# Gate and up of a SwiGLU MLP in seven block products in place of eight, with the output product as a phase of its own

## The chip, the cores and the metric

The kernel runs on one core of one Trainium2 chip. The metric is device time in microseconds (us), as the median of several executions. Beside it stands one profiled execution, from which all durations of single instructions come. Engines are named as in the profile: PE is TensorE (matmuls), PEld its weight load, DVE VectorE, ACT ScalarE, POOL GpSimd and SP SyncE, which here issues DMAs. Each engine takes its instructions in a fixed order; an instruction that waits holds up all behind it on the same engine. Code is written for a scheduler that keeps the order of the program on each engine and moves an instruction only past others that aren't ready.

## The reference, cut to what matters

The input u has L = 2048 tokens of D = 640. Of its two blocks, the first (layer norm, modulation, an S4 convolution by FFT, residual) is not touched by the change. The second is layer norm, modulation and an MLP with F = 1728:

```python
mod = (_silu(c) @ w_mod).reshape(c.shape[0], 6, 1, -1)
sa, ca, ga, sb, cb, gb = ...
x = x + ga * _A_ref(h, ...)                      # the convolution block
h = _layernorm(x, axis=-1) * (1 + cb) + sb
gate = jnp.einsum("bsd,df->bsf", h, w1)          # 640 -> 1728
up = jnp.einsum("bsd,df->bsf", h, w3)
out = jnp.einsum("bsf,fd->bsd", _silu(gate) * up, w2)
x = x + gb * out
```

## The kernel before

**Stages.** The first block takes the start of the execution; at its end the convolution's result lies in DRAM as `zs`. Then comes the MLP, in four quarters q of 512 tokens, each four tiles `xm` of 128 tokens x 640.

**Precision.** Every product of the MLP is three fp32r products: an operand is split into a high part (a cast on ACT) and a low part (operand less high part, on DVE), and hi·hi, hi·lo and lo·hi are added in PSUM (`prod3`, L964 to L969). `split` (L946 to L954) does it for weights and h: ACT's cast is L952, DVE's subtraction L953.

**One f-tile of a quarter** (`mlp`, L986). F is cut in 14 f-tiles: 13 of 128 columns, and f = 13, which holds the last 64 columns of w1 and of w3 side by side. For each, wg, wu and w2 (320 KB each) are loaded by SP (`weight`, L956; `w_get`, L651 and L653), again in each quarter; wg and wu are split (tiles gh, gl, uh, ul); w2 is multiplied with the modulation vector `gbr` on POOL (L1000) and split (wh, wl). Gate `pg` and up `pu` are 15 matmuls each of 128x512 (five blocks of 128 along D, three products each; only `pg` for f = 13), in PSUM pool `psG` of three banks. Then ACT takes silu (L1024), DVE multiplies (`hf`, L1025), and h is split (`hh`, `hl`). `outstep` (L971) multiplies h with w2: 15 matmuls at L981 (10 for f = 13, whose two halves lie on separate partitions), added up over all f in five banks `acc` of pool `psA`. The outstep of f-tile f-1 stands behind gate and up of f-tile f, so its inputs have the time of gate and up to be made. First of all f-tile 0 of quarter 0 orders its products by x's high and low parts (L1009).

**Preparation of the next quarter.** `prep` is a generator; `mlp` takes one step of it per f-tile. Steps are, per tile, `x_mid` (L902): z and x loaded by SP (five z issues, L638, one x issue), eight small matmuls (L914), two additions from PSUM on DVE (L917), the norm's statistics on DVE (L126, L127, L129) and square root on POOL (L131, L132), normalising on DVE (`xn`, L920). Then per 128-block of D, `x_t` (L927): four transposes (L931), ACT's modulation (`xf`, L938) and cast (`xh`, L939), DVE's low part (`xl`, L941). Quarter 0 is prepared by `x_first` (L874), ahead of which TensorE does some matmuls on zeros (`keep_warm`, L868).

**End of a quarter.** `finish` (L1037) runs inside the last outstep: ACT scales acc[4] (`o`, L1040), DVE adds the accumulators to xm (L1043), four transposes (L1047) and four small additions (L1050), and SP stores the tiles (`x_out`).

**What sets the order.** Each engine's queue follows the program, with the scheduler's moves; `issue_after` adds a dependence by hand, `ends` and `last_sum` among them. The room for tiles comes from pools with a fixed number of buffers: two of every weight tile and of every part.

Of the kernel before, what the change touches and what calls it, by code (L numbers as in the profile page):

```python
# [92 lines left out]
def tile_kernel(ctx: ExitStack, tc: tile.TileContext, a):  # L93
# [5 lines left out]
    zs = dram.tile([NDC, NB, 2, NA, DC], F32, name="zs")  # L99

# [539 lines left out]
    def x_tiles(j):  # L640
        return xp.tile([P, D], F32, name=f"xm{j % 4}"), z_tile()
# [7 lines left out]
    def w_get(w, f, name):  # L649
        if name != "w2":  # L650
            nc.sync.dma_start(w, a[name][f])  # L651
        elif f < NFT - 1:
            nc.sync.dma_start(w, a["w2"][f * P:f * P + P, :])  # L653
# [99 lines left out]
    first_w = dict.fromkeys(("wg", "wu", "w2"))  # L753
# [73 lines left out]
    for tk in range(NS + 1, LAG + 8 * NDC + 2):  # L827
# [6 lines left out]
        if tk == NS + 1:  # L834
            tabs.close()
            xp = ctx.enter_context(tc.tile_pool(name="xp", bufs=2))

            xp.tile([P, 8], F32, name="shift_by", bufs=1)
            idle = xp.tile([P, 512], F32R, name="idle", bufs=1)
            G.memset(idle.bitcast(F32), 0.0)  # L840
            for j in range(4):
                early[j] = (xp.tile([P, D], F32, name=f"xm{j}"), early[j][1],
                            xp.tile([P, KD, 6], F32, name="st5", bufs=4))
# [6 lines left out]
    for name in first_w:  # L850
        first_w[name] = xp.tile([P, D] if name == "w2" else [P, KD, P], F32, name="e" + name, bufs=1)
        with tc.issue_after(i1_last[0].ins):
            w_get(first_w[name], 0, name)
# [3 lines left out]
    wq = ctx.enter_context(tc.tile_pool(name="wq", bufs=2, side="right"))  # L857
    mp = ctx.enter_context(tc.tile_pool(name="mp", bufs=2, side="right"))
# [4 lines left out]
    def side_bank(q):  # L863
        return (psG if q else psA).tile([P, 512], F32, name="ps", tag="g" if q else "acc")
# [3 lines left out]
    def keep_warm(n):  # L868

        ps = psA.tile([P, 512], F32, name="ps", tag="acc")  # L870
        for _ in range(n):
            tc.keep_in_program_order(PE.matmul(ps, idle[:, :P], idle, start=True, stop=True))

    def x_first(tiles):  # L874

        keep_warm(IDLE[0])
        pl = psA.tile([P, 4, P], F32, name="pl", tag="acc")
# [15 lines left out]
        V.scalar_tensor_tensor(rs[:, 2, :], mv[:, :, 0], -1.0, rs[:, 1, :], op0=OP.mult, op1=OP.mult)  # L893
        for j, (x, z, st) in enumerate(early):
            xn = xp.tile([P, D], F32, name=f"xn{j}", bufs=1)
# [4 lines left out]
            tiles.append((x, xn))  # L900

    def x_mid(q, tiles):  # L902

        for i in range(4):
            x, z = x_tiles(4 * q + i)
            with tc.issue_after(zlast[0].ins):
                z_load(z, 4 * q + i, range(NDC))
                nc.sync.dma_start(x, a["x"][(4 * q + i) * P:(4 * q + i + 1) * P, :])
            py = [side_bank(q) for _ in range(2)]
            for b in range(4):  # L910
                for hh in range(2):
                    r, c = slice(hh * 64, hh * 64 + 64), slice(b * NA, b * NA + NA)
                    n = ZW[hh]
                    PE.matmul(py[hh][c, :n], i2[r], z[r, b, :n], start=True, stop=True, tile_position=(r.start, c.start))  # L914
            for hh in range(2):
                h = slice(hh * 256, hh * 256 + ZW[hh])
                V.tensor_tensor(x[:, h], py[hh][:, :ZW[hh]], x[:, h], op=OP.add)  # L917
            mean, rstd = ln_stats(xp, x)
            xn = xp.tile([P, D], F32, name=f"xn{i}", bufs=1)
            V.tensor_scalar(xn, x, mean, rstd, op0=OP.subtract, op1=OP.mult)  # L920
            tiles.append((x, xn))
            yield
            yield
# [3 lines left out]
    def x_t(q, tiles, outs):  # L927
        for k in range(KD):
            px = side_bank(q)
            for i in range(4):  # L930
                PE.transpose(px[:, i * P:(i + 1) * P], tiles[i][1][:, k * P:(k + 1) * P], ident)  # L931
            xf = xp.tile([P, 512], F32, name="xf")
            xh = xp.tile([P, 512], F32R, name=f"xh{k}")
            if q == 0 and k % 2 == 0:
                ends[0] = S.activation(xh, px, AF.Identity, scale=modT[:, 1, k:k + 1], bias=modT[:, 0, k:k + 1])
                V.tensor_scalar(xf, px, modT[:, 1, k:k + 1], modT[:, 0, k:k + 1], op0=OP.mult, op1=OP.add)
            else:
                S.activation(xf, px, AF.Identity, scale=modT[:, 1, k:k + 1], bias=modT[:, 0, k:k + 1])  # L938
                ends[0] = S.copy(xh, xf)  # L939
            xl = xp.tile([P, 512], F32R, name=f"xl{k}")  # L940
            ins = V.tensor_tensor(xl, xf, xh.bitcast(F32), op=OP.subtract)  # L941
            ends[1] = ins
            outs.append((xh, xl))
            yield

    def split(pool, src, shape, name, after=None):  # L946
        hi = pool.tile(shape, F32R, name=name + "h")
        lo = pool.tile(shape, F32R, name=name + "l")
        with ExitStack() as order:
            for ins in after or ():  # L950
                order.enter_context(tc.issue_after(ins.ins))
            S.copy(hi, src)  # L952
            V.tensor_tensor(lo, src, hi.bitcast(F32), op=OP.subtract)  # L953
        return hi, lo  # L954

    def weight(q, f, name):  # L956
        if (q, f) == (0, 0):
            return first_w[name]
        w = wq.tile([P, D] if name == "w2" else [P, KD, P], F32, name=name)
# [4 lines left out]
    def prod3(ps, pairs):  # L964
        n = len(pairs)
        for i, ((wh, wl), (xh, xl)) in enumerate(pairs):
            PE.matmul(ps, wh, xh, start=(i == 0), stop=False)  # L967
            PE.matmul(ps, wh, xl, start=False, stop=False)  # L968
            PE.matmul(ps, wl, xh, start=False, stop=(i == n - 1))  # L969

    def outstep(acc, h, w2, f, done=None):  # L971

        if f < NFT - 1:
            terms = [(h[1], w2[0]), (h[0], w2[0]), (h[0], w2[1])]
        else:

            terms = [(h, w2[0]), (h, w2[1])]
        for k in (4, 0, 1, 2, 3):
            for i, (hh, w) in enumerate(terms):
                lhs, rhs = (hh[:, k * P:(k + 1) * P], w[:, :512]) if k < 4 else (w[:, 512:], hh)  # L980
                PE.matmul(acc[k], lhs, rhs, start=(f == 0 and i == 0),  # L981
                          stop=(f == NFT - 1 and i == len(terms) - 1))
# [3 lines left out]
    def mlp(q, tiles, xt, side):  # L986
        acc = None
        prev = None
        for f in range(NFT):
            last = f == NFT - 1  # L990

            after = ends if (q, f) == (0, 1) else last_sum if (q, f) == (0, 0) else None
            wr = weight(q, f, "wg")
            wgs = split(wq, wr, [P, KD, P], "g", after)
            if not last:
                wr = weight(q, f, "wu")
                wus = split(wq, wr, [P, KD, P], "u", after)
            w2r = weight(q, f, "w2")
            with tc.issue_after(zlast[1].ins):
                G.tensor_tensor(w2r[:, :512], w2r[:, :512], gbr, op=OP.mult)  # L1000
            w2s = split(wq, w2r, [P, D], "w", after)
            pg = psG.tile([P, 512], F32, name="pg", tag="g")
            if (q, f) == (0, 0):
                pu = psG.tile([P, 512], F32, name="pu", tag="g")
                for lo in range(2):
                    for k in range(KD):
                        for ps, ws in ((pg, wgs), (pu, wus)):
                            for i in range(1 if lo else 2):
                                PE.matmul(ps, ws[i][:, k, :], xt[k][lo], start=(k + i + lo == 0),  # L1009
                                          stop=(lo == 1 and k == KD - 1))  # L1010
            else:
                prod3(pg, [((wgs[0][:, k, :], wgs[1][:, k, :]), xt[k]) for k in range(KD)])
            if not last and (q, f) != (0, 0):
                pu = psG.tile([P, 512], F32, name="pu", tag="g")
                prod3(pu, [((wus[0][:, k, :], wus[1][:, k, :]), xt[k]) for k in range(KD)])
            if prev is not None:
                if acc is None:
                    acc = [psA.tile([P, 512], F32, name=f"acc{k}", tag="acc") for k in range(KD)]
                outstep(acc, *prev)
            next(side, None)  # L1020
            sg = mp.tile([P, 512], F32, name="sg")
            hf = mp.tile([P, 512], F32, name="hf")
            if not last:
                S.activation(sg, pg, AF.Silu)  # L1024
                V.tensor_tensor(hf, pu, sg, op=OP.mult)  # L1025
                hs = split(mp, hf, [P, 512], "h")
            else:
# [101 lines left out]
```

## Time and profile before

| what | value |
|---|---|
| device time, median of 3 | 1024.65 us |
| lowest and highest of them | 1022.72 and 1025.35 us |
| the profiled execution's own time | 1019.66 us |
| span of that execution in the profile | 1017.5 us |
| mean granted TensorE clock | 0.959 |
| first outstep of the MLP starts | 447.22 us into the span |
| last outstep of the MLP starts | 1005.62 us into the span |

The profile's page has the busy time of each engine first, then the chain of work that ended last, followed back from the last instruction. A view by windows gives, for each stretch of time, the busy time and the number of instructions of each engine, the granted clock, the share of time in which the DMA engines were busy and what they moved. Groups of instructions are given as line, engine, operation, output<-inputs, shapes and count, then busy time in us and mean ns of one, then the idle time of the engine just ahead of them and what ended it. Rows of the chain and of the timelines begin with the start in us and the duration in us.

### The profile page before, as it was taken

The numbers are of one execution on the slowest core, as the hardware profiler recorded it, in microseconds if no ns is written. First come the engines' busy times: TensorE is split into PE (matmuls) and PEld (weight loads), VectorE is DVE, ScalarE is ACT, GpSimd is POOL, SyncE is SP. The second block draws the span as 40 slices with busy tenths as digits, with TensorE's granted clock in tenths as the row PEclk, the third lists the DMA queues.
The fourth block names the chain that finished last, engine by engine and source line by source line (L and its number), as shares of the span: only waits on it lengthen the run. The fifth ranks groups of instructions, "written<-read, shape, count | busy, mean of one in ns | idle before, by whom it ended". The sixth has DMA issues, their size and how long they took to land.

```text
span 1017.5 us, 20360 instructions
## 1 busy us (share of the span) xinstructions
PE 947.8 (93%) x8352; PEld 711.6 (70%) x8352; DVE 606.7 (60%) x1022; ACT 512.9 (50%) x699; POOL 254.7 (25%) x214
## 2 busy tenths in 40 slices
PE   5898797889988989899999999999999999999997
PEld 2544455666666666577788777788777788788886
DVE  4588867888888885665544554534655444533333
ACT  3658676999999953343234333344333344333321
POOL 1443333544445601221111112112111111111110
PEclk9955779999999999999999999999999999999999
DMA  9463496556565679597433455433533333433311
GB/s 266 159 226 121 179 215 200 140 143 161 143 160 129 183 198 283 185 223 165 130 104 91 147 168 137 119 102 91 193 85 98 91 92 98 146 92 99 96 39 52
DMA packets 107041, 146.31 MB, mean 144 GB/s; under 512 B 20836, under 2 KB 62948, under 8 KB 106948
## 3 DMA queue, kind: packets, MB, share of 16 engines
q1 hardware_dynamic: 104420, 140.15, 47.6%
q0 software_dynamic: 1024, 2.49, 0.9%
q10 hardware_dynamic: 1504, 2.36, 0.8%
q8 instruction: 66, 1.08, 0.4%
q14 instruction: 27, 0.22, 0.1%
HBM read 118.76 MB, written 26.21 MB: 142 GB/s over the span
## 4 chain that ended last, share of the span: by engine, by line
PE 72%; ACT 14%; DVE 7%; POOL 3%; DMA 2%; issue 2%; DVEq 0%; ACTq 0%; SPq 0%; POOLq 0%
PE acc L981 17%; PE pg L967 6%; PE pg L968 6%; PE pg L969 6%; PE pu L967 6%; PE pu L969 6%; PE pu L968 6%; ACT cs L119 3%; PE p L554 3%; ACT A L119 3%; ACT ph L119 2%; PE pa L416 2%; ACT L119 2%; PE pu L390 2%; PE pq L428 2%
## 5 line engine op out<-in xcount | busy, mean ns | idle before, releaser
L1000 POOL TENSOR_TENSOR w<-w,gbr 128x512 f32<-128x512 f32 x55 | 82.6, 1502 | 398.3 <-DMA w<-in_w_dram 390.0
L456 POOL TENSOR_TENSOR ph<-thi,iota 128x1024 int32<-128x1024 int32 x40 | 85.4, 2136 | 171.7 <-DVE A L492 78.2
L967 PE MATMUL pg<-xh,gh 128*128 128x512 f32 x275 | 109.8, 399 | 0.1
L952 ACT CAST gh<-wg 128x640 fp32r<-128x640 f32 x55 | 40.2, 731 | 134.0 <-PE pg L968 127.2
L969 PE MATMUL pg<-xh,gl 128*128 128x512 f32 x275 | 107.5, 391 | 0.0
L953 DVE TENSOR_TENSOR gl<-wg,gh 128x640 fp32r<-128x640 f32 x55 | 53.5, 972 | 90.2 <-ACT gh L952 86.5
L968 PE MATMUL pg<-xl,gh 128*128 128x512 f32 x275 | 107.2, 390 | 0.0
L967 PE MATMUL pu<-xh,uh 128*128 128x512 f32 x255 | 99.2, 389 | 0.0
L968 PE MATMUL pu<-xl,uh 128*128 128x512 f32 x255 | 99.2, 389 | 0.0
L969 PE MATMUL pu<-xh,ul 128*128 128x512 f32 x255 | 99.2, 389 | 0.0
L953 DVE TENSOR_TENSOR wl<-w,wh 128x640 fp32r<-128x640 f32 x55 | 46.9, 852 | 85.9 <-ACT wh L952 85.8
L1025 DVE TENSOR_TENSOR hf<-pu,sg 128x512 f32<-128x512 f32 x52 | 36.0, 692 | 103.1 <-PE pu L969 103.1
L554 PE MATMUL p<-uk,s 128*64 128x256 f32 x640 | 79.0, 389 | 13.3 <-PE pa L416 5.6
L952 ACT CAST uh<-wu 128x640 fp32r<-128x640 f32 x51 | 37.3, 731 | 106.4 <-issue 65.2
L981 PE MATMUL acc<-wh,hh 128*128 128x512 f32 x224 | 87.5, 391 | 0.0
L981 PE MATMUL acc<-wl,hh 128*128 128x512 f32 x224 | 87.3, 390 | 0.0
L952 ACT CAST wh<-w 128x640 fp32r<-128x640 f32 x55 | 40.0, 727 | 90.9 <-PE acc L981 89.1
L981 PE MATMUL acc<-wh,hl 128*128 128x512 f32 x208 | 80.9, 389 | 0.0
L554 PEld LDWEIGHTS p<-uk,s 128*64 128x64 f32 x640 | 45.1, 138 | 38.3 <-PE pa L416 8.4
L967 PEld LDWEIGHTS pg<-xh,gh 128*128 128x128 f32 x275 | 51.6, 188 | 17.1 <-issue 5.6
L969 PEld LDWEIGHTS pg<-xh,gl 128*128 128x128 f32 x275 | 51.6, 188 | 11.2
L968 PEld LDWEIGHTS pg<-xl,gh 128*128 128x128 f32 x275 | 51.7, 188 | 10.2
(218 smaller groups left out, 2067.2 us busy)
## 6 DMA issues: line engine op xcount, KB each, us to landing
wg<-in_wg_dram SPq DMA_DIRECT2D x55, 320.0 KB
wu<-in_wu_dram SPq DMA_DIRECT2D x51, 320.0 KB
w<-in_w_dram SPq DMA_DIRECT2D x51, 320.0 KB
us<-u SPq DMA_DIRECT2D x16, 640.0 KB
s<-in_s_dram SPq DMA_DIRECT2D x40, 256.0 KB
i<-in_i_dram SPq DMA_DIRECT2D x40, 256.0 KB
uk<-us SPq DMA_DIRECT2D x32, 256.0 KB
zs<-zt SPq DMA_DIRECT2D x32, 256.0 KB
```

Of the source, the lines that this page charges most:

```text
L119: return tc.keep_in_program_order(S.activation(*args, **kw))
L390: PE.matmul(pu[h][hh * 64:hh * 64 + 64, q, :320], s1r[r], x[r, hh * 320:hh * 320 + 320], start=not (one and h == 0), stop=True, tile_posit ...
L456: hold(G.tensor_tensor(p, bc(thi[:, sl], 2, NPH), bc(iota, 1, SD), op=OP.mult))
L554: keep(PE.matmul(p2[par * 64:par * 64 + 64, pi, c, :], s2[:, pi * 2 + par, c * 64:c * 64 + 64], uk[:, 0:kn + 1:kn, f, :], start=True, stop ...
L952: S.copy(hi, src)
L953: V.tensor_tensor(lo, src, hi.bitcast(F32), op=OP.subtract)
L967: PE.matmul(ps, wh, xh, start=(i == 0), stop=False)
L968: PE.matmul(ps, wh, xl, start=False, stop=False)
L969: PE.matmul(ps, wl, xh, start=False, stop=(i == n - 1))
L981: PE.matmul(acc[k], lhs, rhs, start=(f == 0 and i == 0), stop=(f == NFT - 1 and i == len(terms) - 1))
L1000: G.tensor_tensor(w2r[:, :512], w2r[:, :512], gbr, op=OP.mult)
L1025: V.tensor_tensor(hf, pu, sg, op=OP.mult)
```

## The change

The quarters are taken in pairs, A and B.

**Gate and up.** A few f-tiles ("simple": 0, 1, 2 and 13 in the first pair, 13 in the second) are done for A and for B as before (`plain`). For the other ten and thirteen, four of the five D-blocks form a 2x2 block product: the rows are gate (blocks A11, A12, from wg) and up (A21, A22, from wu), the columns the two quarters. It is done in Strassen and Winograd's form, with seven products of two D-blocks and the fifth D-block added in the plain way (`seven`). Its products have 6, 6, 9, 6, 3, 6, 9 and 9 matmuls, 54 for the pair where `plain` has 60. Four sums of weight blocks, S0 to S3 of 128x256, are made on POOL (`w_sums`) and split (`w_split`) for each f-tile. Sums T1 to T4 of x blocks are made once a pair (`x_sums`: per pair four differences on DVE and four on POOL, each of 128x512) and split (`x_split`). Of the products DVE and ACT make h in `seven`: a copy, six additions from PSUM, two silu, two multiplications.

**Output as a second phase.** All h of A and B are kept in SBUF (in rooms of the pool `tz` and in `h_tile`'s 18 buffers). When the f-tiles of a pair are through, `out` runs the outsteps of A and then of B: each loads w2, multiplies it with `gbr` on POOL, and splits w2 and h there, into the buffers gh, gl, uh and ul (two of each).

**Preparation.** In the first pair's plain f-tiles of A, three steps of the preparation of quarter 1 go with each f-tile. The second pair is prepared in the first pair's output phase (`prepare`): from outstep 3 of A on, one step at a time at outsteps 3, 6, 9, 10, 11, 12, then two steps behind each outstep, through B.

**Else.** x is stored to DRAM (`xs`) as soon as it is normalised and loaded again at outstep 10; the early load of w2, its multiplication and its split are gone; xn lies in rooms of `tz`; raw weights share four buffers `rw`.

```diff
+    xs = dram.tile([NT, P, D], F32, name="xs")
...
-    first_w = dict.fromkeys(("wg", "wu", "w2"))
+    first_w = dict.fromkeys(("wg", "wu"))
...
+    def x_sums(i):
+
+        b11, b21, b12, b22 = xraw["A", i], xraw["A", i + 2], xraw["B", i], xraw["B", i + 2]
+        V.tensor_tensor(b11, b12, b11, op=OP.subtract)
+        G.tensor_tensor(b12, b22, b12, op=OP.subtract)
+        V.tensor_tensor(b22, b22, b11, op=OP.subtract)
+        G.tensor_tensor(b21, b21, b22, op=OP.subtract)
+        for n, t in (("T1", b11), ("T2", b22), ("T4", b21)):
+            xop[n, i] = x_split(f"{n}{i}", t)
...
+    def w_sums(W, names):
+
+        wg, wu, _, _, sums = W
+        for n in names:
...
+            l, r = (lambda: (wu[:, :2], wu[:, 2:4]), lambda: (raw(0), wg[:, :2]),
+                    lambda: (wg[:, :2], wu[:, :2]), lambda: (wg[:, 2:4], raw(1)))[n]()
+            G.tensor_tensor(t[0], l, r, op=OP.subtract if n else OP.add)
+            sums[n] = t
+
+    def w_split(W, names):
+        for n in names:
+            t = W[4][n]
+            S.copy(t[1], t[0])
+            V.tensor_tensor(t[2], t[0], t[1].bitcast(F32), op=OP.subtract)
+
+    def seven(W, hA, hB, nxt):
...
+        b1, b2, b3 = bank(1), bank(0), bank(0)
+        prod3(b1, two(A11, "A"), True, True)
+        m1 = room(0)
+        S.copy(m1, b1)
+        prod3(b2, two(Ss(1), "T2"), True, True)
+        U1 = room(1)
+        V.tensor_tensor(U1, b2, m1, op=OP.add)
+        prod3(b1, two(A12, "A", 2) + [(g4, X("A", 4))], False, True)
+        sg = room(8)
+        S.activation(sg, b1, AF.Silu)
+        prod3(b3, two(Ss(0), "T1"), True, True)
+        t = room(2)
+        V.tensor_tensor(t, b3, m1, op=OP.add)
+        if nxt:
+            w_sums(nxt, (0, 1))
+        prod3(b2, [(u4, X("B", 4))], False, True)
+        b4 = bank(1)
+        prod3(b4, two(Ss(2), "T3"), True, True)
+        V.tensor_tensor(t, b2, t, op=OP.add)
+        V.tensor_tensor(t, b4, t, op=OP.add)
+        if nxt:
+            w_split(nxt, (1, 0))
+        prod3(b3, two(Ss(3), "B", 2) + [(g4, X("B", 4))], False, True)
+        c12 = room(3)
+        V.tensor_tensor(c12, b3, U1, op=OP.add)
+        S.activation(c12, c12, AF.Silu)
+        V.tensor_tensor(hB, t, c12, op=OP.mult)
+        if nxt:
+            w_sums(nxt, (2, 3))
+        prod3(b4, two(A22, "T4") + [(u4, X("A", 4))], False, True)
+        if nxt:
+            w_split(nxt, (2, 3))
+        c21 = room(4)
+        V.tensor_tensor(c21, b4, U1, op=OP.add)
+        V.tensor_tensor(hA, c21, sg, op=OP.mult)
+
+    def outstep(acc, hf, f, pos, done=None):
+
+        w2r = weight(f, "w2")
+        G.tensor_tensor(w2r[:, :512], w2r[:, :512], gbr, op=OP.mult)
+        w2 = [w.rearrange("p k c -> p (k c)") for w in split(w2r.rearrange("p (k c) -> p k c", k=KD), WS, ("gh", "gl"))]
+        h = [wq.tile(WS, F32R, name=n, bufs=2).rearrange("p k c -> p (k c)")[:, :512] for n in ("uh", "ul")]
         if f < NFT - 1:
+            S.copy(h[0], hf)
+            V.tensor_tensor(h[1], hf, h[0].bitcast(F32), op=OP.subtract)
             terms = [(h[1], w2[0]), (h[0], w2[0]), (h[0], w2[1])]
...
+    def out(q, order, h, side):
+        acc = {k: bank(0) for k in (4, 0, 1, 2, 3)}
...
+        for pos, f in enumerate(order):
+            if pos == 10:
+                for i in range(4):
+                    xr.append(x_tile())
+                    nc.sync.dma_start(xr[i], xs[4 * q + i])
+            outstep(acc, h[f], f, pos, finish if pos == NFT - 1 else None)
+            side(pos)
+
+    def prepare(q0, g):
+
+
+        at = [3, 6, 9, 10, 11, 12]
+        for q in (q0, q0 + 1):
+            tiles, got, room2 = [], [], []
+            get = lambda i: got.append(x_get(4 * q + i))
+            mid = lambda i: x_mid(4 * q + i, got[i], room2, tiles, g)
+            for gets, mids in ((0,), ()), ((1,), ()), ((), (0,)), ((2,), (1,)), ((3,), (2,)), ((), (3,)):
+                yield at.pop(0) if at else 0
+                for i in mids:
+                    mid(i)
+                for i in gets:
+                    get(i)
+            for k in ((0, 1, 2, 3, 4) if q % 2 == 0 else (4, 0, 2, 1, 3)):
+                yield 0
+                (turn_b if q % 2 else turn_a)(q, tiles, k, g)
+                if q % 2 and k in (2, 3):
+                    x_sums(k - 2)
...
+        simple = (0, 1, 2, last_f) if pair == 0 else (last_f,)
+        rest = [f for f in range(last_f) if f not in simple]
...
+        for f in simple:
+            hA[f] = h_tile()
+            plain("A", f, hA[f], pair == 0)
+            for _ in range(3):
+                if side:
+                    side.pop(0)()
+        for f in simple:
+            hB[f] = h_tile()
+            plain("B", f, hB[f])
+            if pair == 0 and f < 2:
+                x_sums(f)
+        for i in range(2):
+            x_late(i)
...
+        for n, f in enumerate(rest):
+            nxt = blocks(rest[n + 1]) if n + 1 < len(rest) else None
...
+            seven(W, hA[f], hB[f], nxt)
+            W = nxt
+        order = rest + [f for f in simple]
+        steps = prepare(q0 + 2, 1) if pair == 0 else iter(())
+        due = [next(steps, None)]
+
+        def side_a(pos):
+            for _ in range(2 if pos > 12 else 1):
+                if due[0] is not None and pos >= due[0]:
+                    due[0] = next(steps, None)
+
+        out(q0, order, hA, side_a)
+        out(q0 + 1, order, hB, lambda pos: side_a(14))
```

More of the change, by code (lines that the diff above doesn't have):

```diff
@@ L925, in tile_kernel @@
-    ends = [None, None]
[L927 to L944, printed above, removed]
@@ L949, in split, with x_late @@
+    def x_late(i):
+        xop["T3", i] = x_split(f"T3{i}", xraw["B", i])
+    def split(src, shape, names, after=None, part=slice(None)):
+        hi = wq.tile(shape, F32R, name=names[0], bufs=2)
+        lo = wq.tile(shape, F32R, name=names[1], bufs=2)
         with ExitStack() as order:
```

302 lines of the change are left out of this document (174 added, 128 removed).

## The prediction

> **What bounds the kernel now.** I read the page first: the share of each engine, then the chain that ended last.
>
> ```profile
> span 1017.5 us, 20360 instructions
> PE 947.8 (93%) x8352; PEld 711.6 (70%) x8352; DVE 606.7 (60%) x1022; ACT 512.9 (50%) x699; POOL 254.7 (25%) x214
> PE 72%; ACT 14%; DVE 7%; POOL 3%; DMA 2%; issue 2%; DVEq 0%; ACTq 0%; SPq 0%; POOLq 0%
> ```
>
> TensorE is busy for 93% of the span and carries 72% of the chain. An average hides stages, so next comes the table of windows, for three stretches of the MLP.
>
> ```profile
> 460.00:470.00 10.00, 10.00 (x57) 7.53 (x56) 5.48 (x11) 3.18 (x5) 1.68 (x3) 1.00 1.13 212
> 570.00:590.00 20.00, 18.91 (x96) 14.37 (x95) 13.75 (x22) 6.46 (x10) 3.89 (x3) 1.00 0.63 211
> 880.00:1000.00 120.00, 120.00 (x531) 99.36 (x530) 43.02 (x58) 37.59 (x58) 16.06 (x11) 1.00 0.26 78
> ```
>
> Behind the times stand busy PE, PEld, DVE, ACT, POOL, then granted clock, DMA share and GB/s. In the last quarter PE never stops, at full clock, with DVE at 36%. Only between quarters (570 to 590) does it lose 1.1 us. So in the MLP a matmul less is time less, as long as the others keep up. The chain of waits gives the prices.
>
> ```profile
> 415.70 1.29 POOL ew L1000
> ...
> 447.22 3.40 PE acc L981 x15
> 457.42 3.40 PE acc L981 x15
> 460.81 0.81 PE ps L914 x13
> ...
> 525.16 0.44 PE ps L931 x4
> ...
> 571.60 0.74 ACT gh L952
> 572.36 1.94 DVE gl L953
> 574.34 0.70 DVE hf L1029
> 575.07 0.63 ACT hh L1031
> 575.72 0.70 DVE hh L1032
> 576.46 1.65 PE acc L981 x6
> ...
> 1005.62 4.32 PE acc L981 x19
> 1009.97 1.29 DVE xm L1043 x2
> ```
>
> An outstep of 15 matmuls takes 3.40 us, 0.2267 each; the next begins 10.20 later, 45 matmuls without a gap. One tile's x_mid costs PE 0.81, one turn 0.44.
>
> **The change part by part.** *Removed matmuls.* 23 f-tiles (10 in the first pair, 13 in the second) need 54 products for two quarters instead of 60: 23 x 6 x 0.2267 = **-31.3 us**.
>
> *Removed stalls.* From 447.22 to 1009.94 are 562.7 us. Of the 2440 matmuls 60 lie earlier (f-tile 0, gate and up of 1); 2380 x 0.2267 = 539.5, eleven x_mid 8.9, 60 transposes 6.6, four o-transposes about 2.0: 557.1. The rest, **5.6 us**, is the old stalls, the chain ACT, DVE, ACT, DVE between quarters above all. They go; their successors are counted below.
>
> *Start.* The early w2 and its multiplication (1.29 at 415.70, just ahead of TensorE's warming matmuls) go, and f-tile 0's splits no longer mix with x_mid of the next quarter; but the z loads stand behind four x stores on SP. Bounds -3.5 and +4; I take **-1.5**, nearest to the one row.
>
> *Seven products.* One f-tile of two quarters takes 54 x 0.2267 = 12.2 us. The other engines' prices, from the groups by form:
>
> ```profile
> L953 DVE TENSOR_TENSOR hl<-hf,hh 128x512 fp32r<-128x512 f32 x52 | 36.4, 700 | 1.4 <-ACT hh L952 1.4
> L1025 DVE TENSOR_TENSOR hf<-pu,sg 128x512 f32<-128x512 f32 x52 | 36.0, 692 | 103.1 <-PE pu L969 103.1
> L952 ACT CAST hh<-hf 128x512 fp32r<-128x512 f32 x52 | 32.3, 622 | 20.6 <-DVE hf L1025 20.6
> L941 DVE TENSOR_TENSOR xl<-xf,xh 128x512 fp32r<-128x512 f32 x15 | 10.4, 692 | 7.6 <-ACT xh L939 7.6
> L920 DVE TENSOR_SCALAR xn<-xm,mv,rs 128x640 f32<-128x640 f32 x12 | 7.4, 613 | 10.9 <-POOL rs L132 10.9
> ```
>
> DVE has eight operations of 128x512 at 0.69, four weight-sum splits of half that size, and the low parts of the raw weights (0.83 in the timeline below, and three fifths of it): some 8.3 of 12.2. ACT has about 4.4, POOL four half-sized sums, 2.6 to 3. The tightest waits: TensorE returns to the first bank after six matmuls (1.36 us), and ACT's copy of it takes about 0.6 (as hh); the third is needed nine matmuls (2.04) later, with one 0.69 addition. Each is covered: **0**, from nothing to what a rival says below.
>
> *Outsteps apart.* An outstep now has only itself, 3.40 us, as cover for its inputs: ACT's cast 0.74, DVE's low part 0.83, w2's multiplication on POOL, and the split of h, 0.62 and 0.69. With gh and uh in two buffers the chain just fits. **+1** over some 43 steady outsteps (0 to +13, below).
>
> *First pair, the four plain f-tiles.* The next quarter's preparation ran beside 45 matmuls per step; now three steps go with each 30. Eight half-steps with it are 210 matmuls, four x_mid and five turns, 47.6 + 3.2 + 2.2 = 53 us of PE. DVE has in them about 45: 14 weight splits (11.6), 8 products (5.5), four x_mid at 2.5 (10; rows below), and 25 operations of 128x512 (low parts and sums, 17). 85% of an in-order queue, with DMA as full as in 460 to 470 (share 1.13): bounds 0 and +12, I take **+6**.
>
> *Output phase of the first pair.* Here the whole preparation of the other 1024 tokens is placed, from outstep 10 of A to about outstep 8 of B. What a tile's x_mid does to DVE, and how POOL meets DVE, show in the timelines of DVE and POOL and in the waits.
>
> ```profile
> 583.33 0.83 DVE L953 TENSOR_TENSOR gl<-wg,gh 128x640 fp32r<-128x640 f32 x1 [1.14 <-ACT gh L952]
> ...
> 587.60 0.88 DVE L917 TENSOR_TENSOR xm<-ps,xm 128x256 f32<-128x256 f32 x2
> 588.40 1.16 DVE L953 TENSOR_TENSOR hl<-hf,hh 128x512 fp32r<-128x512 f32 x1
> 589.49 0.48 DVE L126 BATCH_NORM_STATS2 st<-xm 128x6 f32<-128x320 f32 x1
> 589.89 0.47 DVE L127 BATCH_NORM_STATS2 st<-xm 128x6 f32<-128x320 f32 x1
> 590.39 0.21 DVE L129 BATCH_NORM_AGGREGATE mv<-st 128x2 f32<-128x12 f32 x1
> ```
>
> ```profile
> 587.72 1.30 POOL L1000 TENSOR_TENSOR w<-w,gbr 128x512 f32<-128x512 f32 x1 [6.21 <-DVE ul L953]
> 572.33 1.30 POOL L1000 TENSOR_TENSOR w<-w,gbr 128x512 f32<-128x512 f32 x1 [8.68 <-DMA w<-in_w_dram]
> ```
>
> ```profile
> DVE xn L920 <- POOL rs L132: 10.9, 12, 0.9
> ```
>
> x_mid holds DVE for 0.80 + 0.40 + 0.50 + 0.21 + 0.61 = 2.5 us, and 10.9/12 = 0.9 more in which it waits for POOL. In that stretch PE has eleven full outsteps and the short one, eight x_mid, ten turns: 37.4 + 2.3 + 6.5 + 4.4 = 50.6 us. DVE has twelve gl and twelve ul (18.2), eight x_mid (20), ten xl (6.9), four differences and six low parts of them (6.9), and the end of quarter A (about 3.4): 55.4. **So DVE has more work there than TensorE**: 4.8 us over. Its waits come on top: 8 x 0.9 = 7.2 for POOL's square root, about 2 for ACT's copies, and 3 to 5 for z loads. Each tile's z load is five issues, and SP does them in turn behind weight loads and the x stores.
>
> ```profile
> 609.90 2.56 SPq L638 DMA_DIRECT2D A<-zs  x4
> 891.49 0.33 SPq L653 DMA_DIRECT2D w<-in_w_dram  x1
> 894.42 1.60 POOL L1000 TENSOR_TENSOR w<-w,gbr 128x512 f32<-128x512 f32 x1 [14.07 <-DMA w<-in_w_dram]
> ```
>
> (0.64 us an issue; even an unhindered load lands 2.9 us after its issue.) And POOL's sums and multiplications lengthen DVE: gl beside POOL's operation took 1.94 instead of 0.83 (572.36 against 572.33), hl 1.16 (588.40 against 587.72), while the addition from PSUM at 587.60 did not stretch. Of the 16 POOL operations in the stretch (four differences, twelve multiplications) I let half hit, at 1.1 each: 9. In the order of the instructions DVE has the four differences, eleven low parts and a gl, about 10.6 us, ahead of the ul on which TensorE waits about outstep 7 of B; cover there is one or two outsteps. Bounds: 5 (DVE always busy, no wait) and 36 (all waits, all 16 collisions); the sum 4.8 + 7.2 + 2 + 4 + 9 = 27, of which the first outsteps' slack of an input ahead takes about 2: **+25**.
>
> *Boundaries.* Five remain: into the seven products, out of them, A to B in each pair, and the second pair's start, each with a chain like 571.60 to 576.46, which cost 1.1. Chains now start from a PSUM result not yet split: **+5** (0 to +10).
>
> *Clock.* A TensorE that waits long starts slow, as at the MLP's start; the windows:
>
> ```profile
> 417.00:419.00 2.00, 1.94 (x6) 1.64 (x7) 1.53 (x5) 0.73 (x1) 0.00 (x0) 0.70 0.17 43
> 419.00:421.00 2.00, 2.00 (x9) 1.06 (x11) 0.00 (x0) 0.00 (x0) 0.00 (x0) 0.50 0.19 52
> 421.00:423.00 2.00, 2.00 (x35) 1.04 (x35) 0.26 (x2) 0.00 (x0) 0.00 (x0) 0.94 0.00 1
> ```
>
> After PE had little to do, about 4 us passed near half clock, 2 us lost. I take one or two such places: **+3** (0 to +6).
>
> The Trainium skill, "TensorE: Matmul & The Clock Gate", section "What's actually happening", says that TensorE drops to half clock after about 3.4 us idle and needs as long to come back; the rows above agree with the return. By it, as an estimate, each stall of over 3.4 us costs about 1.7 more. The Trainium skill, "SBUF — State Buffer", section "SBUF: two separate sides", speaks against this change: VectorE and GpSimd share a port pair as an exclusive lock, held for the whole instruction, and the loser blocks; gl at 1.94 beside 1.30 on POOL agrees. By it every meeting costs up to 1.3, and what this would do is the second rival.
>
> *Sum.* -31.3 - 5.6 - 1.5 + 0 + 1 + 6 + 25 + 5 + 3 = **+1.6** on the profiled execution's 1019.66, thus 1021.3. The median, 1024.65, is 5.0 above that execution; the forecast for it is 1024.65 + 1.6, rounded **1026 us**: about no change.
>
> **The rivals.** *1, the preparation stays hidden: 1005 us.* TensorE loses only DVE's overload and its waits for the square root (4.8 + 7.2 = 12), 2 in the plain f-tiles, 4 at boundaries, 1 of clock: -38.4 + 19 = -19.4. For it: DVE is at 36% in the last quarter and 60% over all, and inputs two buffers ahead soak up some of each wait. Against: the in-order queue and the block of 10.6 us in front of one ul.
>
> *2, slower: POOL's multiplication stands in every outstep, 1038 us.* gh and uh have two buffers, so the chain from one release to the next start has 3.40 us. If w2's multiplication takes the ports just between gl and the low part of h, it is 0.74 + 0.83 + 1.30 + 0.69 = 3.56, and four handovers of 0.02 to 0.04 (as from 574.30 to 574.34): 3.7. 0.3 late at each of 43 outsteps is +13, for 12 more than in the sum. It decides from the point at which this chain passes 3.40. For it: w2 lands 2.9 us after its issue, and its room in the four raw buffers is released by a gl, so the multiplication comes due as the next gl runs. Against: h is already there, so its cast can go first and ul before gl.
>
> *3, the change does not do what it says: 1054 us.* If weight sums hold DVE up, the four reuses of a bank (copy, first sum, two additions) open a gap each; 23 x 4 x 0.3 = 27.6 on top of the sum. Against: 8.3 of 12.2 us on DVE, and POOL's operations are half-sized there.
>
> **How the numbers follow.** The forecast's case, with a net of -8 to +8 (1017 to 1033) by the bounds of its middle terms, gets 0.45; rival 1 0.27, rival 2 0.22, rival 3 0.06. Range 1004 to 1043: it takes in rival 1, and rival 2 with 5 us of its terms' spread; outside lie rival 3 and the tails, under 2 in 10. 0.3%, about 3 us, is what a measurement here can tell from no change. Of the forecast's case 0.14 lies below -3, 0.17 within, 0.14 above. Faster 0.14 + 0.27 = 0.41; same 0.17; slower 0.14 + 0.22 + 0.06 = 0.42.
>
> **What would show it.** In the profile after: the seven products as 12.2 us a period with PE full (else rival 3); steady outsteps 3.40 apart (3.7: rival 2); between outstep 10 of A and 8 of B in the first pair PE idle for some 25 us, released by DVE's low part of h, DVE full there (12 or less: rival 1); 2 to 6 us of idle in the plain stage. I am wrong if the idle time of that output phase is released by DMA instead, if TensorE loses time in the stage of seven products, or if DVE's operations beside POOL keep their short durations.

## The result and the profile after

The changed kernel takes 1040.45 us (median of 4, 1039.77 to 1042.94) where the kernel before took 1023.69 beside it: ratio **1.017, 95% interval 1.0141 to 1.0199**. It is slower by some 17 us. The forecast was 1026, about no change, in a range of 1004 to 1043.

The page of the changed kernel, its first two lines:

```profile
span 1038.0 us, 20686 instructions
PE 938.6 (90%) x8214; PEld 694.3 (67%) x8214; DVE 728.1 (70%) x1230; ACT 532.2 (51%) x784; POOL 334.9 (32%) x314
```

138 matmuls are gone and TensorE's busy time has sunk by 9 us only, in a span 20.5 us longer. VectorE has 121 us more, GpSimd 80. The page's chain is of no use here: it reaches back only 55 us from the end. So the MLP was cut by its stages. The windows, changed kernel: plain f-tiles, seven products, output of the first pair; then f-tile 13 and seven products, and output of the second.

```profile
436.24:500.23 63.99, 59.39 (x297) 43.16 (x296) 47.03 (x75) 30.18 (x52) 17.39 (x20) 0.97 0.61 186
500.23:622.63 122.40, 122.40 (x541) 101.35 (x540) 78.96 (x135) 46.12 (x88) 30.08 (x37) 1.00 0.17 49
622.63:766.02 143.39, 118.06 (x588) 86.96 (x586) 93.50 (x136) 50.96 (x83) 46.22 (x46) 0.92 0.53 154
766.02:931.96 165.94, 165.94 (x734) 137.39 (x732) 110.96 (x194) 64.79 (x125) 45.67 (x56) 1.00 0.23 74
931.96:1030.55 98.59, 95.08 (x410) 76.16 (x409) 62.14 (x64) 34.08 (x55) 34.95 (x23) 0.98 0.32 97
```

The same of the kernel before, from its first MLP matmul to the end of the same stretch of the last outstep:

```profile
430.16:1009.94 579.78, 575.44 (x2702) 464.95 (x2701) 271.27 (x392) 206.08 (x314) 91.86 (x79) 1.00 0.40 116
```

579.78 has become 594.31, 14.5 more. (The other 6.1 us of the two spans lie ahead of the MLP; see below.) With 0.2267 for a matmul, 0.81 for a tile's x_mid, 0.44 for a turn and 0.5 for four o-transposes, each stage has a floor:

| stage | floor | took | lost |
|---|---|---|---|
| plain f-tiles (210 matmuls, 4 x_mid, 5 turns) | 53.0 | 64.0 | 11.0 |
| seven products, first pair (540 matmuls) | 122.4 | 122.4 | 0 |
| output, first pair (410, 8 x_mid, 10 turns) | 104.8 | 143.4 | **38.6** |
| f = 13 and seven products, second pair (732) | 165.9 | 165.9 | 0 |
| output, second pair (410) | 93.4 | 98.6 | 5.2 |

The seven products run without one gap. What they save is lost again where they aren't: in the output phase of the first pair. TensorE's waits in that phase, longest first (changed kernel, 622.63 to 766.02: engine, tile and line that waited, for whom; us, times, longest):

```profile
PE ps L1139 <- DVE ul L1129: 17.5, 4, 13.4
PE ps L931 <- DMA A<-zs: 3.5, 3, 1.3
PE ps L1139 <- ACT gh L998: 3.1, 1, 3.1
PE ps L956 <- DVE A L939: 0.7, 2, 0.5
```

They make up all but 0.5 of the 25.3 us in which TensorE idles there. The first row is an outstep that waits for the low part of its h, once for 13.4 us, until 743.8. VectorE's timeline just before (changed kernel; T1, T2 and T4 are the sums, T3 is a block of x itself):

```profile
728.66 1.67 DVE L949 TENSOR_TENSOR T10l<-s,T10h 128x512 fp32r<-128x512 f32 x1 [0.32 <-ACT T10h L948]
730.25 1.75 DVE L949 TENSOR_TENSOR xB2l<-s,xB2h 128x512 fp32r<-128x512 f32 x1
731.92 1.75 DVE L980 TENSOR_TENSOR s<-s,s 128x512 f32<-128x512 f32 x1
733.59 0.68 DVE L982 TENSOR_TENSOR s<-s,s 128x512 f32<-128x512 f32 x1
734.19 0.68 DVE L949 TENSOR_TENSOR T31l<-s,T31h 128x512 fp32r<-128x512 f32 x1
734.79 1.75 DVE L949 TENSOR_TENSOR xB3l<-s,xB3h 128x512 fp32r<-128x512 f32 x1
736.46 1.76 DVE L949 TENSOR_TENSOR T20l<-s,T20h 128x512 fp32r<-128x512 f32 x1
...
739.95 1.88 DVE L999 TENSOR_TENSOR gl<-rw,gh 128x640 fp32r<-128x640 f32 x1
...
742.95 0.68 DVE L1129 TENSOR_TENSOR ul<-h,uh 128x512 fp32r<-128x512 f32 x1
```

and GpSimd's in the same stretch:

```profile
728.49 1.29 POOL L981 TENSOR_TENSOR s<-s,s 128x512 f32<-128x512 f32 x1 [4.59 <-DVE T30l L949]
729.74 3.38 POOL L1124 TENSOR_TENSOR rw<-rw,gbr 128x512 f32<-128x512 f32 x2
734.35 1.65 POOL L983 TENSOR_TENSOR s<-s,s 128x512 f32<-128x512 f32 x1 [1.23 <-DVE s L982]
735.96 1.71 POOL L981 TENSOR_TENSOR s<-s,s 128x512 f32<-128x512 f32 x1
739.50 1.65 POOL L983 TENSOR_TENSOR s<-s,s 128x512 f32<-128x512 f32 x1 [1.83 <-DVE s L982]
```

Read the two together. One operation of 128x512 on VectorE takes 0.68 alone and 1.75 when a GpSimd operation runs beside it; POOL's own take 1.65 in place of 1.29. The block of sums stands in VectorE's queue ahead of the `ul` at 742.95, which TensorE needs, and six of the operations there are stretched.

The third row shows a second way in which GpSimd holds TensorE up. It is the wait until 708.95 for `gh`; ScalarE's cast of `gh` had itself waited for w2's multiplication, and that stood in GpSimd's queue behind a square root which waited for VectorE's statistics (changed kernel, GpSimd and then ScalarE):

```profile
706.09 0.19 POOL L132 TENSOR_TENSOR rs<-mv,epst 128x1 f32<-128x1 f32 x1 [6.57 <-DVE mv L130]
706.36 0.55 POOL L133 TENSOR_TENSOR rs<-rs,epst 128x1 f32<-128x1 f32 x1
706.87 1.26 POOL L1124 TENSOR_TENSOR rw<-rw,gbr 128x512 f32<-128x512 f32 x1
```

```profile
708.17 0.72 ACT L998 CAST gh<-rw 128x640 fp32r<-128x640 f32 x1 [5.06 <-POOL rw L1124]
```

Half clock follows each of the three long waits (3.65, 3.08 and 13.4 us, ending at 680.5, 709.0 and 743.8); behind the one of 0.90 us at 669.4 the clock stayed full. Granted clock is the third column from the right (changed kernel):

```profile
680.00:690.00 10.00, 9.20 (x47) 6.27 (x48) 5.78 (x14) 2.37 (x4) 0.74 (x2) 0.83 0.47 165
700.00:710.00 10.00, 5.60 (x44) 3.09 (x43) 6.61 (x14) 1.62 (x3) 3.25 (x4) 0.89 0.80 224
710.00:720.00 10.00, 10.00 (x43) 7.21 (x45) 5.95 (x7) 2.40 (x5) 6.18 (x6) 0.77 0.88 257
730.00:740.00 10.00, 0.35 (x2) 0.00 (x0) 10.00 (x11) 4.96 (x9) 6.94 (x5) 0.75 0.00 0
740.00:750.00 10.00, 6.22 (x17) 4.98 (x18) 4.97 (x7) 2.29 (x5) 3.71 (x3) 0.56 0.22 66
```

TensorE's busy time times the missing share of clock is 1.6 + 0.6 + 2.3 + 0.1 + 2.7 = 7 us in these windows. A busy row is no full row. Of the 38.6 us lost in this phase, 25.3 are idle and some 7 are half clock. Most of the other 6 follow from TensorE's work being cut into smaller pieces: x_mid now runs in two halves apart (at 666.49 and 669.37, for one) and takes some 1.2 us a tile instead of 0.81, and a matmul of the outstep beside such a break takes 0.3 to 0.4 us to the next start instead of 0.23.

### The profile page after: what moved, and what is told of

Same layout as the page of the kernel before. It is cut to its first block, busy times and chain, and to the rows that moved or that the text cites. A ratio compares the mean times of both kernels' runs of the same rounds, so it can differ in the third digit from the quotient of the medians.

```text
span 1038.0 us, 20686 instructions
## 1 busy us (share of the span) xinstructions
PE 938.6 (90%) x8214; PEld 694.3 (67%) x8214; DVE 728.1 (70%) x1230; ACT 532.2 (51%) x784; POOL 334.9 (32%) x314
## 5 line engine op out<-in xcount | busy, mean ns | idle before, releaser
L998 ACT CAST gh<-rw 128x640 fp32r<-128x640 f32 x89 | 64.8, 728 | 169.8 <-POOL rw L1124 74.9
L999 DVE TENSOR_TENSOR gl<-rw,gh 128x640 fp32r<-128x640 f32 x89 | 80.4, 904 | 68.8 <-ACT gh L998 68.0
L1124 POOL TENSOR_TENSOR rw<-rw,gbr 128x512 f32<-128x512 f32 x56 | 80.6, 1441 | 139.8 <-DMA rw<-in_w_dram 134.5
L555 PE MATMUL p<-uk,s 128*64 128x256 f32 x640 | 79.2, 390 | 13.3 <-PE pa L417 5.6
L1139 PE MATMUL ps<-gh,uh 128*128 128x512 f32 x224 | 89.9, 402 | 0.0
L1139 PE MATMUL ps<-gl,uh 128*128 128x512 f32 x224 | 89.4, 400 | 0.0
L1139 PE MATMUL ps<-gh,ul 128*128 128x512 f32 x208 | 83.9, 403 | 0.0
L555 PEld LDWEIGHTS p<-uk,s 128*64 128x64 f32 x640 | 45.3, 139 | 38.6 <-PE pa L417 8.4
L482 DVE TENSOR_TENSOR E<-A,cs 128x1024 f32<-128x1024 f32 x40 | 49.3, 1233 | 1.7 <-ACT A L120 1.7
L489 DVE TENSOR_TENSOR A<-A,ph 128x1024 f32<-128x1024 f32 x40 | 49.9, 1248 | 0.0
L524 PE MATMUL pt<-s,K 128*64 128x128 f32 x640 | 47.8, 293 | 0.5 <-ACT uk L123 0.5
L506 PE MATMUL pk<-E 128*32 128x64 f32 x1280 | 46.9, 233 | 1.2 <-DVE E L485 0.6
```

The lines of the kernel that those rows point to most:

```text
L482: keep(V.tensor_tensor(EC[s][:, :, 1:3, :], AA[s][:, :, 1:3, :], mid(cs[s]), op=OP.mult))
L489: keep(V.tensor_tensor(A[:, :, 1:3, :], A[:, :, 1:3, :], mid(ph[s]), op=OP.mult))
L506: keep(PE.matmul(pk[dq * 32:dq * 32 + 32, g, :], x[:, g * 4 + dq, 1, :], x[:, g * 4 + dq, 0:3:2, :], start=(st == 0), stop=(st == 1), tile ...
L524: keep(PE.matmul(pt[c * 64:c * 64 + 64, g, :], kk[:, g, :], s1[:, c, :], start=True, stop=True, tile_position=(0, c * 64)))
L555: keep(PE.matmul(p2[par * 64:par * 64 + 64, pi, c, :], s2[:, pi * 2 + par, c * 64:c * 64 + 64], uk[:, 0:kn + 1:kn, f, :], start=True, stop ...
L998: S.copy(hi[:, part], src[:, part])
```

## The experiments

**Theory V**, from the prediction: VectorE's queue holds the low part of h back, in one block above all. **Theory L**: it is GpSimd's operations, above all w2's 56 multiplications, which hold VectorE up wherever they meet. **Theory D**: the loads of z come late. Beside each time stands its ratio to the kernel before. That kernel took 1020.7 to 1021.7 us beside the runs below and 1023.69 beside the changed kernel, so a difference of some 3 us between the changed kernel's time and one of these shows nothing by itself.

**The sums spread out.** The scheduler had put the sums ahead of the outsteps' inputs since they were ready first, so they are held by hand, behind one more outstep's `ul` each; the turns of quarter B are held in the same way.

```diff
...
-                    x_sums(k - 2)
+                    for part in range(2):
+                        yield at_b.pop(0)
+                        with tc.issue_after(last_ul[0].ins):
+                            x_sums(k - 2, (part,))
...
```

> The changed kernel with the x sums of the second pair in four parts, each held on its engines behind the low part of h of one more outstep (outsteps 4 to 12 of B), instead of in one block. Theory V (VectorE's queue: the block of sums and low parts ahead of one low part of h is what TensorE waits for): the idle 13.4 us at 743.8 goes but for 1 or 2, and about 2.5 us of half clock behind it: 1040.5 - 14 = 1026, within 4. Theory L (GpSimd's operations hold VectorE up wherever they meet): the pieces still meet multiplications, half comes back elsewhere: 1034. Theory D (the loads of z are late): 1039 or more.

Measured: 1032.9 us, ratio 1.0122 (1.0095 to 1.0150). It was nearer to L than to V. The stage is 137.6 instead of 143.4 us; TensorE's wait at the block is 4.2 instead of 13.4, but its pieces still meet multiplications, as VectorE and then GpSimd of this kernel show:

```profile
730.71 1.75 DVE L949 TENSOR_TENSOR xB2l<-s,xB2h 128x512 fp32r<-128x512 f32 x1
732.38 1.88 DVE L1002 TENSOR_TENSOR gl<-rw,gh 128x640 fp32r<-128x640 f32 x1
734.18 0.68 DVE L1132 TENSOR_TENSOR ul<-h,uh 128x512 fp32r<-128x512 f32 x1
```

```profile
730.20 3.38 POOL L1127 TENSOR_TENSOR rw<-rw,gbr 128x512 f32<-128x512 f32 x2
```

**No multiplication of w2** in the outsteps (this kernel leaves the MLP's output modulation out).

```diff
-        G.tensor_tensor(w2r[:, :512], w2r[:, :512], gbr, op=OP.mult)
```

> The changed kernel without w2's multiplication on GpSimd in the outsteps (this leaves the MLP's output modulation out). Theory V: the block of sums keeps its four GpSimd differences and its length but for some 3 collisions: 1040.5 - 6 = 1034, idle at the block still about 10. Theory L: 56 multiplications gone, VectorE's low part of h 0.69 again instead of 1.8 in each outstep, outsteps 3.40 instead of 3.44 and the stage of preparation 12 shorter: 1024. Theory D: 1039 or more.

Measured: 1024.69, ratio 1.0029 (0.9999 to 1.0058): L's number. That it is so near is partly luck, since the stage of preparation became 9.7 us shorter where L had 12, and V's block is there still: TensorE waits 10.2 us at it. The steady outsteps of the second pair are 3.40 apart again (3.44 in the changed kernel), for this reason; VectorE, changed kernel and then this one:

```profile
1002.79 0.83 DVE L999 TENSOR_TENSOR gl<-rw,gh 128x640 fp32r<-128x640 f32 x1 [0.90 <-ACT gh L998]
1003.54 1.78 DVE L1129 TENSOR_TENSOR ul<-h,uh 128x512 fp32r<-128x512 f32 x1
```

```profile
984.69 0.82 DVE L999 TENSOR_TENSOR gl<-rw,gh 128x640 fp32r<-128x640 f32 x1 [1.97 <-ACT gh L998]
985.43 0.68 DVE L1128 TENSOR_TENSOR ul<-h,uh 128x512 fp32r<-128x512 f32 x1
```

This edit takes two things away at once: the meetings with VectorE, and the multiplication as a step ahead of `gh`. No run parts them. In the stage of preparation VectorE has as many operations as before and is busy for 80.2 us instead of 93.5: 13.3 us of stretching are gone. TensorE's waits for `gh` there sink from 3.1 to 0.7 us.

**Both edits.**

> Both edits (the output modulation left out again). Theory V: 1026 - 4 = 1022. Theory L: 1016. Theory D: 1038. If the two edits take away the same stall, the sum of their gains is not reached.

Measured: 1011.8, ratio 0.9899 (0.9861 to 0.9937), better than either theory had. The output stage of the first pair, for the sums spread, the multiplication left out, and both:

```profile
619.77:757.36 137.59, 119.67 (x588) 88.29 (x587) 94.93 (x138) 51.07 (x83) 45.22 (x45) 0.93 0.57 162
```

```profile
620.95:754.66 133.71, 116.58 (x587) 86.93 (x586) 80.22 (x136) 50.88 (x83) 14.40 (x23) 0.94 0.56 165
```

```profile
620.43:741.54 121.11, 112.80 (x587) 83.65 (x586) 80.94 (x138) 51.44 (x85) 15.69 (x24) 0.99 0.63 183
```

-5.8, -9.7 and together -22.3 us (each from one profiled execution). The two causes strengthen each other: a block hurts as long as its operations are stretched, and a stretched operation hurts where the queue has no slack. With both gone the granted clock is 0.99 in place of 0.92. Theory D falls as the main cause, though its waits are real: 1.2 to 4.7 us in this stage of the changed kernel and these three runs.

**The kernel before, again**, for the 6.1 us ahead of the MLP. From 154 to 168 us the changed kernel's clock was 0.53, in code that the change leaves alone.

> The kernel before, profiled again. In the profile of the changed kernel the clock fell to half from 155 to 168 us, in code that the change does not touch, and the MLP began 6 us later. If that is chance of an execution, it may show here too, with a span of some 1022 to 1024; if it hangs on the changed kernel, the clock here stays at 1.00 from 150 to 200 and the span at 1017 to 1019.

Measured: 1014.93 in a single run, clock 1.00 in that stretch, first MLP matmul at 428.45. That seemed to speak for the change as the cause. So one more run was made on it: the kernel **before with a DRAM tensor more** and four stores into it.

```diff
+    xs = dram.tile([NT, P, D], F32, name="xs")
...
+        for j, (x, z, st) in enumerate(early):
+            nc.sync.dma_start(xs[j], x)
```

> The kernel before with one more DRAM tensor of 5 MB and four stores of x into it at the start of the MLP, for the fall of the clock at 155 us that all profiles of the changed kernel's family show, and neither of the two of before. If the place of things in DRAM sets it, it shows here: first MLP matmul at 433 to 436 instead of 428 to 430, time 4 to 5 us above before. If not, the time is that of before within 2.

Measured: 1020.84, ratio 1.0002 (0.9984 to 1.0021), so no change of time; yet its profiled execution has the fall, and that of the next experiment, of the changed kernel's family, has none. The windows of this kernel, then of that one:

```profile
154.00:168.00 14.00, 8.96 (x42) 4.18 (x44) 8.00 (x13) 4.90 (x6) 5.05 (x3) 0.67 0.55 183
```

```profile
154.00:168.00 14.00, 10.23 (x140) 6.19 (x142) 9.02 (x15) 7.14 (x9) 3.42 (x2) 1.00 0.57 196
```

So the fall comes with and without the change: of the ten profiles of the changed kernel and its variants eight have it, of the three of the kernel before and its variant one. Whether the change makes it more frequent, so few profiles can't tell. Two profiles differ by up to 8 us in where the MLP begins (428 to 437) in either family. Of the 20.5 us between the two spans 14.5 lie in the MLP, where the change is; the medians' 17 may contain some of the rest. Why the fall comes in one execution and not in another was not settled.

**w2 multiplied once**, a version that computes everything: beside the seven products of the first pair, stored to DRAM, and loaded from there by all outputs; sums spread as above.

```diff
...
+    def w_scale(f):
+
+        if held:
+            g, w = held.pop()
+            nc.sync.dma_start(ws[g], w)
+        if f is not None:
+            w = x_tile()
+            w_get(w, f, "w2")
+            G.tensor_tensor(w[:, :512], w[:, :512], gbr, op=OP.mult)
+            held.append((f, w))
...
```

> The whole computation: e1_apart, and w2 is multiplied on GpSimd once, in 14 multiplications beside the seven products of the first pair, stored to DRAM and loaded from there in all four outputs. Theory L (GpSimd holds VectorE): the outsteps are as in e4_apart_nomul, 3.40 us each, and the total is its 1012, within 3. Rival: the 14 multiplications now hold VectorE beside the seven products, whose tightest waits have 0.6 to 1.2 us of cover; that stage grows from 122.4 us by up to 10, total up to 1022.

Measured: 1015.43, ratio **0.9957 (0.9935 to 0.9978)**: faster than before. The output stage is 120.4 us, near the 121.1 without the multiplications, and the stage of seven products keeps its 122.4 although VectorE is busy there for 83.8 us instead of 79.0: the rival is out. By L: VectorE is cheap again as soon as GpSimd does its work elsewhere.

**Inputs of the outsteps one ahead.**

```diff
...
-            outstep(acc, h[f], f, pos, finish if pos == NFT - 1 else None)
+            cur, ins = ins, nxt and out_in(*nxt)
+            outstep(acc, cur, pos, finish if pos == NFT - 1 else None)
...
```

> e5_once with the inputs of each outstep (load and split of w2, split of h) traced one outstep ahead, so that those of B's first stand in front of the end of A in VectorE's queue. Theory V: the waits for VectorE's low part of h at the A to B boundaries (2.4 us in the second pair, 1.8 of half clock behind it, and part of the first pair's 9.7 us outstep) go: 5 less than e5_once, about 1007. Rival: the boundary waits for the accumulators' banks themselves, then nothing changes (within 1).

Measured: 1012.11, ratio **0.9926 (0.9901 to 0.9951)**, the best whole version. V holds as to the place: in the second pair the end of A and the first outstep of B take 6.24 and 3.90 us instead of 8.80 and 4.88 in the last kernel, and TensorE's wait of 2.4 us there is gone. Its size, 3 us, is less than 5, and the intervals of this kernel and the last overlap.

**Sums of the first pair one plain f-tile later.**

```diff
...
-            if pair == 0 and f < 2:
-                x_sums(f)
+            if pair == 0 and f in (1, 2):
+                with tc.issue_after(last_lo[0].ins):
+                    x_sums(f - 1)
...
```

> e6_ahead, and the sums of the first pair held one plain f-tile of B later, behind its weights' low parts. Theory V: the waits of 0.5, 0.7 and 1.9 us in B's first plain f-tile, which low parts of x end behind the sums in VectorE's queue, go, and the half clock behind them (about 1.5): 4 less than e6_ahead, about 1003. Rival: sums come too late for the first of the seven products, which then waits: within 1 of e6_ahead, or slower.

Measured: 1014.22, ratio 0.9944 (0.9925 to 0.9962): nothing won. A wait of 5.3 us appears at the end of the plain f-tiles: w2's multiplications for DRAM, which the scheduler had moved up there, now meet the sums. VectorE and GpSimd of this kernel:

```profile
494.27 1.74 DVE L950 TENSOR_TENSOR T21l<-s,T21h 128x512 fp32r<-128x512 f32 x1
496.15 1.54 DVE L950 TENSOR_TENSOR T41l<-s,T41h 128x512 fp32r<-128x512 f32 x1
497.61 0.68 DVE L1071 TENSOR_TENSOR h<-ps,s 128x512 f32<-128x512 f32 x1
```

```profile
494.03 1.44 POOL L987 TENSOR_TENSOR s<-s,s 128x512 f32<-128x512 f32 x1
495.43 1.71 POOL L1030 TENSOR_TENSOR xm<-xm,gbr 128x512 f32<-128x512 f32 x1
```

**Normalising on ScalarE**, in the changed kernel and in the best version.

```diff
...
-        V.tensor_scalar(xn, x, mean, rstd, op0=OP.subtract, op1=OP.mult)
+        S.activation(xn, x, AF.Identity, scale=rstd, bias=nb[:, 1:2])
...
```

> The changed kernel with the normalising of x_mid on ScalarE instead of VectorE (GpSimd makes the bias with two more operations of one column), in both pairs' preparation. Theory V: VectorE loses 12 operations of 0.6 to 1.6 us and the waits for GpSimd's square root (8.7 us in the output phase), but the block of sums stays: 1040.5 - 6 = 1034, within 4. Rival: ScalarE's queue takes the wait over and holds the casts of w2 and h behind it: within 2 of 1040, or slower.

> e6_ahead with the same edit. VectorE is busy for 73% of the stretch of preparation there and waits 7.1 us for GpSimd's square root. Theory V: 4 to 7 less than e6_ahead, 1005 to 1008. Rival (ScalarE takes the wait over): within 2 of 1012, or slower.

Measured: 1035.87, ratio 1.0149 (1.0107 to 1.0192). By the times it is 4.6 us less than the changed kernel, but the two intervals overlap for the most part, so a gain is not shown; the block's 13.2 us are still there. And 1017.27, ratio 0.9966 (0.9943 to 0.9988), where the rival wins. In the second, ScalarE stands waiting in VectorE's place, and the casts of w2 queue behind it (waiter, releaser; us, times, longest):

```profile
ACT A L945 <- POOL nb L941: 22.4, 8, 4.4
```

**Plain f-tiles in the second pair**, the output a phase of its own as in the changed kernel:

```diff
...
-        simple = (0, 1, 2, last_f) if pair == 0 else (last_f,)
+        simple = (0, 1, 2, last_f) if pair == 0 else tuple(range(NFT))
...
```

> The changed kernel with all 14 f-tiles of the second pair in the plain way, the output still as a phase of its own (the sums of x are made but not used). Theory V, by the count of matmuls: 13 x 6 x 0.2267 = 17.7 more, 1058, and the stage of gate and up of the second pair 183.6 us instead of 165.9. Rival 3 of the prediction (the seven products lose in waits what they save): the same 1040 within 4.

Measured: 1058.47, ratio 1.0371 (1.0335 to 1.0406), 18.0 more than the changed kernel; the stage of gate and up of the second pair took 183.64 us instead of 165.94, 17.7 more:

```profile
767.03:950.67 183.64, 183.64 (x811) 152.12 (x810) 63.90 (x90) 52.78 (x82) 7.81 (x5) 1.00 0.36 113
```

In their stage the seven products give exactly what the count of matmuls says.

## Why the prediction was half right

The measured 1040.45 lies in the range, in the 0.42 given to "slower"; the likeliest case, 1017 to 1033, missed it. Term by term of the sum:

- *Removed matmuls, -31.3; seven products, 0.* Right. Two stages of 540 and 732 matmuls have no gap, and 13 f-tiles made plain cost 17.7 in their stage, as counted, and 18.0 in all. Rival 3 is out.
- *Removed stalls, -5.6.* Right, or a little small: 579.8 less a floor of 571.5 (2440 matmuls, 12 x_mid, 15 turns and the o-transposes) is 8.3, the first f-tile's included.
- *Start, -1.5.* Not readable: where the MLP begins varies by 8 us from execution to execution.
- *Outsteps apart, +1.* Right: 3.44 against 3.40. **Rival 2** named the mechanism that works in each of them, the multiplication between gl and the low part of h, and its price was wrong: 0.04, not 0.3. The multiplication begins while gl still runs, so of its 1.3 to 1.6 us only some 1.1 stand in the chain (ul 1.78 instead of 0.68): 0.73 + 0.83 + 1.78 and the handovers are 3.44. Its time, 1038, was near by accident.
- *Output phase, +25.* The idle time is right: from 650 to 750 us TensorE idles 25.3 us, and 17.5 of the phase's idle time ends with a low part of h, as forecast.

```profile
650.00:750.00 100.00, 74.67 (x396) 51.71 (x395) 69.16 (x107) 35.21 (x58) 34.45 (x36) 0.88 0.59 171
```

  Its make-up is less so. VectorE was busy for 69% of that stretch, not all the time: the loss is not a surplus of work (4.8 in the sum) but order and stretching. Half of the idle is the one block, which the prediction had named, at outstep 7 of B; 12 operations of VectorE were stretched by about 1 us, for which it had 8 at 1.1.
- *Clock, +3.* **This is the first term that was mis-sized.** The prediction counted one or two places; there were three in this phase alone, with 7 us of half speed, and others in the plain f-tiles and at the last A to B. A wait of 3 to 13 us must be counted with the slow stretch behind it.
- *Plain f-tiles, +6.* **The second:** 11.0 (its bound was 12), of which 4.6 is idle and 1.7 half clock. Of the idle time 2.6 comes by the same order: sums ahead of the low parts of x that TensorE is waiting for.
- *Boundaries, +5.* About right: the last A to B alone lost 5.5 (9.95 + 5.12 for matmuls and transposes of 9.6), the two into and out of the seven products nothing.

So the mechanism was right, VectorE's queue beside the outsteps. The stages lost 54.8 us where the sum's terms for them come to 40; the 15 us between lie in clock, plain stage and the part of the output phase that is not idle. That GpSimd's multiplications are the greater lever, some 15 us by themselves, was in the prediction as 9 us of collisions and in a rival; that it and the block strengthen one another was not foreseen at all.

The Trainium skill, "SBUF — State Buffer", section "SBUF: two separate sides", says that the loser of the shared ports blocks for the winner's whole instruction. The traces agree as far as they show it: 0.68 becomes 1.75 beside an operation of 1.3 to 1.7. By that rule alone, not by VectorE's share of busy time, the change could have been doubted.

## What to carry to other kernels

Work saved on the bound engine is kept only where the others' work lies beside it; moved preparation has to be priced at the place where it lands, in the order of the in-order queue, and with what GpSimd does at that moment. Before adding sums on a second engine that stretches the first one's operations (0.68 to 1.75 us here), count what that engine already does there: here a multiplication done 56 times could be done 14 times in a quieter stage, and this, a hand-held order and inputs made one outstep ahead turned 1.7% slower into 0.7% faster. And count half clock behind every wait of some microseconds (3.1 to 13.4 us here).

## What the runs showed of the hardware that was not expected

- VectorE's normalising (`tensor_scalar`, one tensor operand in SBUF) was stretched beside GpSimd like the operations with two: 1.57 instead of 0.61. The additions from PSUM kept their time: 19 of those of `b4` onto `t` (128x512, L1104 of the changed kernel) began while GpSimd made a weight sum, and each took 0.69 as the other four did.
- The clock fell at 155 us after waits of only 0.54 and 2.06 us with little work between; in the kernel before, at the same place, it did not after waits of 1.04 and 1.56. TensorE's timeline of the changed kernel, then of before:

```profile
155.10 0.59 PE L337 MATMUL pm<-misc,part 128*128 128x1 f32 x2 [2.06 <-DVE part L286]
```

```profile
155.34 0.38 PE L336 MATMUL pm<-misc,part 128*128 128x1 f32 x2 [1.56 <-DVE part L285]
```

  From there on 16 matmuls of 128x256 took 3.29 us instead of 1.95.
